# Mask matmuls of the first batch behind both units' scores on 64 rows, and late attention results placed by VectorE and small transfers

## The chip, the cores and the metric

One core of a Trainium2 chip. The metric is device microseconds of one execution; a run's time is the median of its repeated executions. The parts of the core that matter here: TensorE (PE, with PEld for its weight loads), VectorE (DVE), ScalarE (ACT), GpSimd (POOL) and SyncE (SP), whose queue issues most of the transfers. The granted clock is the share of TensorE's full clock that the profile records; "half clock" is a stretch in which it was 0.50. All runs told here were of the fast state, and all gave correct results.

## The reference, cut to what matters

Block-sparse attention, followed by a Fourier mix and a two-layer network, on 4 batches of 8 heads, 768 positions and head size 64.

```python
def _attn_ref(q, k, v, sampled_blocks):           # (4, 8, 768, 64) each
    scores = scale * np.matmul(q, k.transpose(0, 1, 3, 2))
    mask = ...   # near blocks, first and last block row and column, sampled blocks (32 x 32)
    scores = np.where(mask, scores, -1000000000.0)
    attn = softmax(scores)                        # cut: written out in the original
    return np.matmul(attn, v)

# x = attention result as (4, 768, 512)
def _moe_ref(x, w_ch1, w_ch2):
    u = x + np.real(np.fft.fft(np.fft.fft(x, axis=1), axis=2))
    un = (u - mean(u)) / sqrt(var(u) + 1e-6)      # cut
    return u + np.maximum(un @ w_ch1, 0.0) @ w_ch2
```

## The kernel before

Two heads make a pair; there are 4 pairs to a batch, 16 in all. A unit is one key tile of 128 by half of the queries (384) for both heads of a pair. A step does two units: their scores, the exponentials, and the values of the step before. A batch is 24 steps. While the attention of one batch runs, the Fourier mix and the network of the batch before are threaded in.

In the first batch (`n < NP`) the mask is not yet there as a tile, so it is added on TensorE: two bfloat16 matmuls of 24 rows (`NB`) put a large negative number on masked blocks. Later batches multiply by a mask tile on VectorE.

```python
def scores(u):
    ...
    s = ps_s.tile([P, 2, 512], FP32, tag="s", name="s")      # two PSUM buffers
    for i in range(2):                                       # two heads, 64 rows each
        nc.tensor.matmul(s[:, i, 0:HS], kT[D * i:D * i + D, c * P:(c + 1) * P],
                         qT[D * i:D * i + D, half * HS:(half + 1) * HS],
                         start=True, stop=n >= NP)
    if n < NP:
        for i in range(2):
            nc.tensor.matmul(s[:, i, 0:HS], of_k[D * i:D * i + NB, c * P:(c + 1) * P],
                             off_q[D * i:D * i + NB, half * HS:(half + 1) * HS],
                             start=False, stop=True)
    return s
```

The values come out transposed (`o`, head size by queries). ACT copies them to SBUF, TensorE transposes them back (`xt`), and ACT copies that into `x`. I call this a placing; each half of a pair has one.

```python
def values(u):
    ...                                                      # matmuls into o
    if c == C - 1:
        oT = sum_p.tile([P, HS], FP32, tag="oT", name="oT")
        nc.scalar.copy(out=oT, in_=o_of.pop((n, half)))

def place(n, half):
    ...
    xt, at = ps_t.tile([P, 512], FP32, tag="t", name="xt"), bank("t")   # the only buffer "t"
    for c in range(T):                                                  # T = 3
        nc.tensor.transpose(xt[:, c * P:(c + 1) * P], oT[:, c * P:(c + 1) * P], ident)
    nc.scalar.copy(out=x_of[b, half][:, :, j * P:(j + 1) * P], in_=...)
```

In the first batch ACT and DVE also unpack the weights, 32 rounds (`w_round`: two ACT instructions, five DVE instructions, about 3 us of DVE each), and each step issues its short jobs (transposes of q and k, placings) when the kernel's own model thinks that their inputs are ready:

```python
while short and (s in (2, 5) or len(short) > 1 or phase == 0 or r == 0):
    ready = [i for i in short if max(i[1], min(free[i[0]])) <= when["PE"] + 0.1]
    if not ready and s not in (2, 5) and r > 0:
        break
    ...
```

## Time and profile before

| | before |
|---|---|
| time, median of 3 runs | 1109.58 us (1108.61 to 1111.27) |
| span of the profiled run | 1108.8 us, mean granted clock 0.988 |
| PE / DVE / ACT busy | 96% / 60% / 35% |
| longest wait of PE | 4.04 us at 25.27 us |
| first step of the second batch (start of its scores) | 135.41 us |

PE sets the time, so one asks of every change what it takes from PE, and what then stands just behind PE. "Busy" is a share of the whole span.

### The profile page before, as it was taken

How to read it: one execution, taken by the hardware profiler on the slowest of the kernel's cores; microseconds unless marked ns; L12 is line 12 of the kernel's file. 1: busy time of each engine (PE TensorE's matmuls, PEld its weight loads, DVE VectorE, ACT ScalarE, POOL GpSimd, SP SyncE). 2: the span in 40 equal slices, each digit the busy share in tenths (PEclk: the TensorE clock that was granted, in tenths of full speed). 3: DMA queues.
4: the chain of work that ended last, by engine and by line, in shares of the span. 5: the costliest groups of instructions: out<-in, count | busy, mean ns of one | idle time of the engine just before them, and what ended most of it. 6: DMA issues, size and time to landing. Idle time of an engine off the chain costs nothing.

```text
span 1108.8 us, 12273 instructions
## 1 busy us (share of the span) xinstructions
PE 1065.3 (96%) x4370; PEld 537.9 (49%) x4370; DVE 670.6 (60%) x1227; ACT 389.8 (35%) x786; POOL 271.2 (24%) x302
## 2 busy tenths in 40 slices
PE   7999988998899999999999999999999999999996
PEld 4333333443455545444444545444444555568675
DVE  5688878497864535564558635555456446575563
ACT  5788755565202102253443212344330202120210
POOL 1000078487200001245537000343540000000000
PEclk9999999999999999999999999999999999999998
DMA  7557322022000000212210000211000000100001
GB/s 237 151 161 234 109 53 59 15 44 43 1 1 1 1 1 19 62 24 39 43 29 15 0 1 1 55 46 29 1 1 1 0 1 20 38 1 1 1 16 44
DMA packets 86689, 44.28 MB, mean 40 GB/s; under 512 B 74318, under 2 KB 79452, under 8 KB 86620
## 3 DMA queue, kind: packets, MB, share of 16 engines
q1 hardware_dynamic: 84732, 42.62, 14.5%
q10 hardware_dynamic: 1856, 0.79, 0.3%
q8 instruction: 36, 0.59, 0.2%
q14 instruction: 33, 0.27, 0.1%
q0 software_dynamic: 32, 0.01, 0.0%
HBM read 37.11 MB, written 6.29 MB: 39 GB/s over the span
## 4 chain that ended last, share of the span: by engine, by line
PE 83%; DVE 10%; ACT 2%; issue 2%; DMA 1%; POOL 1%; SPq 0%; ACTq 0%; DVEq 0%; POOLq 0%
PE y L1017 23%; PE z L961 14%; PE s L541 10%; PE o L585 8%; PE yp L961 7%; PE yy L1080 6%; PE xp L961 3%; DVE e L562 3%; PE zp L774 1%; PE sp L632 1%; PE zp L745 1%; DMA out_dram<-x 1%; PE xt L603 1%; PE tp L483 1%; DVE w_sb L452 1%
## 5 line engine op out<-in xcount | busy, mean ns | idle before, releaser
L572 POOL TENSOR_TENSOR acc<-acc,e 128x384 f32<-128x384 f32 x192 | 197.4, 1060 | 89.5 <-DVE e L562 88.9
L541 PE MATMUL s<-qT,kT 64*128 64x384 f32 x768 | 164.4, 531 | 15.2 <-DVE e L562 11.0
L562 DVE TENSOR_TENSOR e<-s,mask 128x768 f32<-128x768 f32 x144 | 131.1, 949 | 65.0 <-ACT s L560 62.9
L585 PE MATMUL o<-e,vr 128*64 128x384 f32 x768 | 148.0, 507 | 0.0
L560 ACT ACTIVATE s<-s 128x768 f32<-128x768 f32 x144 | 109.5, 791 | 89.3 <-PE s L541 88.1
L1020 DVE TENSOR_TENSOR x<-y,x 128x512 f32<-128x512 f32 x72 | 49.8, 691 | 146.8 <-PE y L1017 146.7
L1017 PE MATMUL y<-w_sb,hA 128*128 128x512 f32 x288 | 129.5, 595 | 1.1 <-ACT zs L776 1.1
L1017 PE MATMUL y<-w_sb,hB 128*128 128x512 f32 x288 | 128.5, 596 | 1.0 <-DVE x L1020 1.0
L572 POOL TENSOR_TENSOR acc<-e 128x384 f32<-128x384 f32 x48 | 50.0, 1063 | 231.3 <-DVE e L562 189.1
L541 PEld LDWEIGHTS s<-qT,kT 64*128 64x128 f32 x768 | 62.4, 187 | 85.1 <-DVE e L562 37.9
L966 DVE TENSOR_TENSOR hA<-z,hA 128x384 f32<-128x384 f32 x64 | 35.7, 558 | 97.5 <-PE z L961 97.5
L961 PE MATMUL z<-unT,t 128*128 128x384 f32 x256 | 93.0, 486 | 0.0
L837 POOL TENSOR_SCALAR st<-st 128x1 f32<-128x1 f32 x24 | 6.7, 277 | 348.1 <-DVE st L836 347.7
L1017 PEld LDWEIGHTS y<-w_sb,hB 128*128 128x128 f32 x288 | 53.3, 190 | 67.3 <-issue 65.6
L585 PEld LDWEIGHTS o<-e,vr 128*64 128x64 f32 x768 | 47.4, 138 | 75.9 <-issue 72.3
L1017 PEld LDWEIGHTS y<-w_sb,hA 128*128 128x128 f32 x288 | 52.9, 190 | 62.9 <-issue 58.5
L970 ACT ACTIVATE hA<-hA 128x384 f32<-128x384 f32 x64 | 33.5, 523 | 119.9 <-DVE hA L966 119.5
L961 PEld LDWEIGHTS z<-unT,t 128*128 128x128 f32 x256 | 48.6, 190 | 33.9
L970 ACT ACTIVATE hB<-hB 128x384 f32<-128x384 f32 x64 | 33.5, 523 | 86.1 <-DVE hB L966 86.1
L961 PE MATMUL xp<-unT,w_sb 128*128 128x384 f32 x128 | 48.5, 503 | 1.3 <-DVE x L1020 0.7
L981 ACT COPY hA<-xp 128x384 f32<-128x384 f32 x32 | 15.3, 479 | 95.8 <-PE xp L961 95.8
L961 PE MATMUL z<-t,w_sb 128*128 128x384 f32 x128 | 46.6, 487 | 0.9 <-DVE t L923 0.9
(197 smaller groups left out, 1409.1 us busy)
## 6 DMA issues: line engine op xcount, KB each, us to landing
wraw<-in_moe_w_ch_dram SPq DMA_DIRECT2D x32, 512.0 KB
vr<-in_v_dram SPq DMA_DIRECT2D x30, 192.0 KB
qr<-in_q_dram SPq DMA_DIRECT2D x48, 64.0 KB
kr<-in_k_dram SPq DMA_DIRECT2D x14, 192.0 KB
qb<-in_q_dram SPq DMA_DIRECT2D x28, 96.0 KB
kb<-in_k_dram SPq DMA_DIRECT2D x28, 96.0 KB
out_dram<-x SPq DMA_DIRECT2D x16, 128.0 KB
out_dram<-x SPq DMA_DIRECT2D x8, 256.0 KB
```

What stands on the lines that cost most here:

```text
L541: nc.tensor.matmul(s[:, i, 0:HS], kT[D * i:D * i + D, c * P:(c + 1) * P], qT[D * i:D * i + D, half * HS:(half + 1) * HS], start=True, stop ...
L560: nc.scalar.activation(out=s[:, :, 0:HS], in_=s[:, :, 0:HS], func=ACT.Exp, scale=scale)
L562: nc.vector.tensor_tensor(out=e, in0=s[:, :, 0:HS], in1=m.broadcast_to([P, 2, HS]), op=ALU.mult)
L572: nc.gpsimd.tensor_add(out=acc, in0=e_of[u - 1][:, i, :] if c == 1 else acc, in1=e[:, i, :])
L585: nc.tensor.matmul(o[D * i:D * i + D, :], vt[:, i, c, :], e[:, i, :], start=(c == 0), stop=(c == C - 1))
L961: nc.tensor.matmul(to, a[:, k, :], c[:, k, :], start=(k == 0), stop=(k == ND // 2 - 1))
L966: tt(out=to, in0=ps, in1=a, op=ALU.add)
L970: nc.scalar.activation(out=h, in_=h, func=ACT.Relu)
L981: nc.scalar.copy(out=h11, in_=x)
L1017: nc.tensor.matmul(y, hs[0, half][:, l, m * P:(m + 1) * P], w2_sb[:, 4 * r + l, :], start=(l == 0), stop=(l == 3))
L1020: nc.vector.tensor_tensor(out=x[:, m, :], in0=y, in1=x[:, m, :], op=ALU.add)
L1080: nc.tensor.matmul(ps, a[:, k, :], c[k // 2][:, k % 2, :] if isinstance(c, list) else c[:, k, :], start=(k == 0), stop=(k == 3))
```

## The change

Three things, with one aim, fewer microseconds on PE:

1. The mask matmuls of a step stand behind the scores of both units and use 64 rows like the scores (the rows that hold no mask are zeroed once).
2. The transposes of the first pair's second half of q are issued one step earlier (`sl > 1`).
3. From the third batch on, three pairs of four are placed without PE: DVE transposes `o` in blocks of 32 by 32, and 16 small transfers per half put the blocks into `x`. For their sake the loads of q and k are issued earlier in the step.

```diff
+    nc.vector.memset(of_k, 0.0)
+    nc.vector.memset(off_q, 0.0)
...
-    def scores(u):
+    def scores(us):
...
+        for u in us:
+            ...                                   # score matmuls of both units, as before
+        for u, s in got if n < NP else ():
+            for i in range(2):
+                rows = slice(D * i, D * i + D)
+                nc.tensor.matmul(s[:, i, 0:HS], of_k[rows, c * P:(c + 1) * P], off_q[rows, queries],
+                                 start=False, stop=True)
...
+            if in_blocks(n):
+                nc.vector.transpose(out=oT, in_=o_of.pop((n, half)))
...
+    def in_blocks(n):
+        return n > 2 * NP and n % NP > 0
+
+    def place_blocks(n, half):
+        b, j = pairs[n]
+        oT = o_of.pop((n, half)).rearrange("p (c t d) -> p c t d", t=P // BLK, d=BLK)
+        for g in range(P // BLK):
+            for t in range(P // BLK):
+                nc.sync.dma_start(
+                    out=x_of[b, half][BLK * t:BLK * t + BLK, :, j * P + BLK * g:j * P + BLK * (g + 1)],
+                    in_=oT[BLK * g:BLK * g + BLK, :, t, :])
...
-            if not ready and s not in (2, 5) and r > 0:
+            if not ready and s not in (2, 5) and r > 0 and sl > 1:
...                                               # load_q, load_k moved ahead of the short jobs
```

More of the change, by code (lines that the diff above doesn't have):

```diff
@@ L531 @@
     SLOT = 2
-    def scores(u):
-        n, w = divmod(u, UP)
-        half, c = divmod(w, C)
+    def scores(us):
+        n, w = divmod(us[0], UP)
+        half = w // C
         qT, kT = turned[n, 0], turned[n, 1]
-        s = ps_s.tile([P, 2, 512], FP32, tag="s", name="s")
-        busy("PE", 0.72 if n >= NP else 1.0, max(e_at.get(u - SLOT, 0.0), z_at[u % 2]))
-        s_at[u] = when["PE"] + HOP
-        for i in range(2):
-            nc.tensor.matmul(s[:, i, 0:HS], kT[D * i:D * i + D, c * P:(c + 1) * P],
-                             qT[D * i:D * i + D, half * HS:(half + 1) * HS],
-                             start=True, stop=n >= NP)
-        if n < NP:
-            for i in range(2):
-                nc.tensor.matmul(s[:, i, 0:HS], of_k[D * i:D * i + NB, c * P:(c + 1) * P],
-                                 off_q[D * i:D * i + NB, half * HS:(half + 1) * HS],
+        queries = slice(half * HS, (half + 1) * HS)
+        got = []
+        for u in us:
+            c = u % C
+            s = ps_s.tile([P, 2, 512], FP32, tag="s", name="s")
+            got.append((u, s))
+            busy("PE", 0.72, max(e_at.get(u - SLOT, 0.0), z_at[u % 2]))
+            s_at[u] = when["PE"] + HOP
+            for i in range(2):
+                rows = slice(D * i, D * i + D)
+                nc.tensor.matmul(s[:, i, 0:HS], kT[rows, c * P:(c + 1) * P], qT[rows, queries],
+                                 start=True, stop=n >= NP)
+        for u, s in got if n < NP else ():
+            c = u % C
+            busy("PE", 0.25)
+            s_at[u] = when["PE"] + HOP
+            for i in range(2):
+                rows = slice(D * i, D * i + D)
+                nc.tensor.matmul(s[:, i, 0:HS], of_k[rows, c * P:(c + 1) * P], off_q[rows, queries],
                                  start=False, stop=True)
-        return s
+        return got
     def weigh(u, s):
@@ L590, in values @@
             oT = sum_p.tile([P, HS], FP32, tag="oT", name="oT")
-            nc.scalar.copy(out=oT, in_=o_of.pop((n, half)))
-            oT_at[n, half] = busy("ACT", 0.5, when["PE"] + HOP) + HOP
+            if in_blocks(n):
+                nc.vector.transpose(out=oT, in_=o_of.pop((n, half)))
+                oT_at[n, half] = busy("DVE", 0.5, when["PE"] + HOP) + HOP
+            else:
+                nc.scalar.copy(out=oT, in_=o_of.pop((n, half)))
+                oT_at[n, half] = busy("ACT", 0.5, when["PE"] + HOP) + HOP
             o_of[n, half] = oT
@@ L1244, in slot @@
         if sl < B * SB:
-            for u, ps in [(u, scores(u)) for u in units]:
+            for u, ps in scores(units):
                 weigh(u, ps)
@@ L1256, in slot @@
                 e_of.pop(u)
+        if s == 3 and n + 2 < len(pairs):
+            load_q(n + 2)
+        if s == 0 and 0 < n < len(pairs) - 1:
+            load_k(n + 1)
         reuse = n % NP == 0 and phase >= 2
@@ L1264, in slot @@
                 at = when["PE"] + LEAVES
-            short.append(("t", at, lambda: place(n, 0)))
+            if in_blocks(n):
+                place_blocks(n, 0)
+            else:
+                short.append(("t", at, lambda: place(n, 0)))
         if 0 < sl <= B * SB and s == 0 and n % NP != 1:
-            short.append(("t", oT_at[n - 1, 1], lambda: place(n - 1, 1)))
+            if in_blocks(n - 1):
+                place_blocks(n - 1, 1)
+            else:
+                short.append(("t", oT_at[n - 1, 1], lambda: place(n - 1, 1)))
         if sl < B * SB and n % NP == 1 and s == 1:
@@ L1313, in slot @@
                     fn(*args)
-        if s == 3 and n + 2 < len(pairs):
-            load_q(n + 2)
-        if s == 0 and 0 < n < len(pairs) - 1:
-            load_k(n + 1)
         w_loads()
```

## The prediction

> **What bounds the kernel now.** I read the page's busy shares and slices first, then the chain of waits, then the timeline of each stage. The page says that TensorE (PE) is the bound: 96% busy, and the chain that ended last is 83% PE and 10% VectorE (DVE).
>
> ```profile
> PE 1065.3 (96%) x4370; PEld 537.9 (49%) x4370; DVE 670.6 (60%) x1227; ACT 389.8 (35%) x786; POOL 271.2 (24%) x302
> ...
> PE   7999988998899999999999999999999999999996
> ...
> DVE  5688878497864535564558635555456446575563
> ```
>
> So what leaves PE counts in full, except where another engine stands just behind it. In the first five slices (27.7 us each) DVE is that engine: 8 or 9 tenths. This is the first batch, in which DVE also unpacks the weights. The timeline of its start shows the one long wait of PE in the run:
>
> ```profile
> 18.61 0.43 DVE L450 TENSOR_SCALAR wraw<-wraw 128x512 uint32<-128x512 uint32 x1 [8.89 <-ACT wraw L449]
> ...
> 24.57 0.55 DVE L492 COPY qT<-tp 128x128 f32<-128x128 f32 x3
> ...
> 25.27 1.65 PE L541 MATMUL s<-qT,kT 64*128 64x384 f32 x4 [4.04 <-DVE qT L492]
> ```
>
> PE has transposed the second half of q at 18.56, but the copy stands on DVE behind two weight rounds (18.61 to 24.57). PE idles 4.04 us, and its next score matmuls take 1.65 us where others take 0.92. From 32.3 us to 135.4 us PE then has no wait over 0.31 us. One unit's scores, its mask matmuls, the next unit's, and what follows:
>
> ```profile
> 43.93 0.92 PE L541 MATMUL s<-qT,kT 64*128 64x384 f32 x4
> 44.78 0.34 PE L546 MATMUL s<-at_q,at_k 24*128 24x384 bf16 x2
> 45.04 0.92 PE L541 MATMUL s<-qT,kT 64*128 64x384 f32 x4
> 45.89 0.34 PE L546 MATMUL s<-at_q,at_k 24*128 24x384 bf16 x2
> 46.16 1.51 PE L585 MATMUL o<-e,vr 128*64 128x384 f32 x8
> ```
>
> Read the differences of the starts, since the durations overlap: two units take 46.16 - 43.93 = 2.23 us. In the second batch, without mask matmuls, two units take 146.30 - 144.81 = 1.49 us:
>
> ```profile
> 144.81 1.56 PE L541 MATMUL s<-qT,kT 64*128 64x384 f32 x8
> 146.30 0.55 PE L659 MATMUL st<-ident,sums 128*128 128x128 f32 x3
> ```
>
> The first batch ends with DVE late: it works without a gap until its first masked product, and PE waits for that 1.51 us.
>
> ```profile
> 140.19 1.80 DVE L562 TENSOR_TENSOR e<-s,mask 128x768 f32<-128x768 f32 x2
> 141.18 1.78 PE L541 MATMUL s<-qT,kT 64*128 64x384 f32 x8 [1.51 <-DVE e L562]
> ```
>
> From 415 to 840 us, where the other half of the change lies, PE is busy 417.89 of 425 us and DVE 230.51: only PE matters there.
>
> **What the Trainium skill says.** "TensorEngine Tiling (Array Packing)", Key Properties, has it that a change of the tiling mode, not of the tile, drains the engine. The trace agrees: a run of two score passes before a mask takes 0.85 us (43.93 to 44.78), a run of four takes 1.49, so an inner pass is 0.32 and the two ends of a run cost 0.21 together, about 0.10 each. "TensorE: Matmul & The Clock Gate", Part 1, gives half clock after an idle window of about 3.4 us; here the 4.04 us wait is followed by matmuls at half speed until about 31 us. "VectorE: DVE Perf Modes", The three transpose paths, says that DVE transposes only within 32x32 blocks; hence the 16 transfers per half, which put the blocks in place. "DMA: Bandwidth & Descriptors", Rules for kernel authors, warns that transfers under 64 KB are mostly overhead; these are 12 KB. No transfer like them is in this trace, so their time is my least certain input.
>
> **The change, part by part.**
>
> *Mask matmuls.* 24 steps of two units. Now the mask pair has 24 rows, a different mode from the scores' 64, so a step has four runs. Afterwards it is one run of 64 rows: four score passes, then two mask pairs. A mask pair at the end of a run takes 0.26 (45.89 to 46.16), thus about 0.16 inside one. If nothing but rows matters, a step takes 1.49 - 0.10 + 0.16 + 0.26 = 1.81: 0.42 saved. If the step from f32 to bf16 drains as well, 1.91: 0.32 saved; if each mask's weights wait too, 2.01: 0.22. I take 0.35, 8.4 us over the batch. The exponentials on ScalarE (ACT) of the first unit start about 0.9 us later; the values that read them come a step later, so this should be hidden.
>
> *The early copy.* The order of instructions shows that the q transpose moves ahead of the third step's scores, and its copy ahead of all weight rounds on DVE. The 4.04 us go, and half clock from 25.3 to 31 us, 5.7 us at half speed: 2.9 us. A new wait comes: this transpose now directly follows another in the same single PSUM buffer, which ACT must empty first (six copies, 1.03 us, which start after the exponentials). Laying the recorded durations in the new order gives the third step's scores at about 17.9 us instead of 16.33, then the fifth step's at about 26.9, against 32.33 plus the 0.48 of a placing transpose that now stands ahead of it: some 6.0 us gained, the masks of the first four steps included. The other 20 steps bring 20 x 0.35 = 7.0: PE would reach the second batch 13.0 us earlier.
>
> *What DVE makes of this.* From its weight round at 62.08 us to the masked product at 140.19 DVE has only about 4.8 us idle (gaps of 1.55, 1.44 and 1.80); before, it has gaps of 4.37, 4.14 and 3.13. All are waits for ACT or PE, which come earlier too, so most of them close; but its first weight round starts some 1.5 us later, behind the square of q on ACT. I put DVE's end at 127.5 to 128.5 us, 12 us earlier; PE waits there 2.5 us instead of 1.5. Gain at the second batch: 11.8 us. Its PE, DVE and ACT orders are otherwise unchanged, so the shift is kept.
>
> *Late placing.* Six pairs, two halves: 12 placings. Each takes 3 PE transposes away, 0.48 us (156.23 to 156.71), 5.7 us in all, and waits in front of some of them, the largest 1.42 us at 578 and 0.85 us here:
>
> ```profile
> 837.16 0.52 PE L603 MATMUL xt<-ident,oT 128*128 128x128 f32 x3 [0.85 <-DVE sums L616]
> ```
>
> I count 1.5 us of these. 24 ACT copies of 0.48 us go too, which PE does not wait for. Added: 12 DVE transposes of 128x384; the one of 128x768 takes 968 ns, so about 0.5 us each, 6 us on an engine a little over half busy; and 192 transfers. A 1 to 63 row transfer holds the queue for about 0.26 to 0.32 us, so I estimate 16 in about 5.5 us, landing 2 us later. The next use of the same buffer is three steps, over 20 us, later. Loads stand in the same queue, but the change issues q and k ahead of them, and v is needed a pair later. The last placing matters most: it stores into x at the end of the attention part. DVE scales x there:
>
> ```profile
> 842.24 1.29 DVE L674 TENSOR_TENSOR x<-x,r 128x512 f32<-128x512 f32 x2
> 844.91 0.69 DVE L1020 TENSOR_TENSOR x<-y,x 128x512 f32<-128x512 f32 x1 [1.38 <-PE y L1017]
> 845.52 1.89 DVE L674 TENSOR_TENSOR x<-x,r 128x512 f32<-128x512 f32 x3
> ```
>
> Only the second half of x is concerned, from the middle of the last line on, 846 us; with values done at 835.5, the transpose at 836.1 and 7.5 us of transfers it is there at about 844. PE has second-layer matmuls of the batch before to do meanwhile. No cost, narrowly.
>
> *Sum.* 11.8 + 5.7 + 1.5 = 19.0. I take off 1 us for half clock: waits of 2.48 and 2.18 us in the second batch were followed by 3.4 us windows at half speed, and the DVE wait at the batch's border may now be one of those. Net 18 us: 1109.6 - 18 = 1091.6 us.
>
> **Rivals.** (1) *DVE becomes the bound of the first batch and swallows the masks' gain.* For: 87.11 us busy in the 103 us from 34 to 137 and late already at the end. Against: 10 us of gaps that are waits for others. If they stay open, the first batch gains only some 7 us, and the time is about 1096. (2) *bf16 behind f32 drains anyway, and ACT gets bursts.* ACT is 84.55 of 103 us busy and takes two exponentials in a row later than now; the two score buffers could make PE wait for it. Worth 3 to 5 us: 1095. (3) *The small transfers hold up the queue or the last x.* If one costs 0.6 us of queue as the q loads do (3.82 us for 6), 16 take 10 us, the last x is 3 to 4 us late, and PE loses some of it: 1094. (4) *All works, DVE's gaps close fully and waits at xt go too*: 14 + 8 = 22 us, 1087.5, right at the border of 2%.
>
> **Range and chances.** The sure pieces are the start's wait (at least 4 us) and 12 placings (5.7 us): no less than about 10 us. Everything together gives 22 to 23. Hence 1087 to 1098 for 8 in 10. 2% is 22.2 us, 1087.4: only rival 4 gets there, 0.13. Slower by 2% needs a long new wait that nothing suggests: 0.01.
>
> **What would show it.** In the first batch, two units' scores with masks 1.8 to 1.9 us apart from start to the values' start (2.0 or more: drains remain); no wait of 4 us before 26 us, one of about 1 us at the transpose near 17 us, and no half clock; the first step without masks at 122 us instead of 135.4, and the PE wait at its second step at 2 to 4 us, for DVE e (10 us would mean rival 1). DVE's gaps between 28 and 123 us, about 17 us in all now, shrink to 8 or less. The placing transposes fall from 96 to 60, and the stretch from 415 to 840 us becomes 6 to 7 us shorter. A DVE or PE wait for the transfers near the end of attention would prove rival 3. I am wrong in the main if the first batch gains under 8 us.

## The result, and the profile after

| | before | after |
|---|---|---|
| time, median (same rounds, 4 runs each) | 1110.09 us (1108.61 to 1111.27) | 1093.09 us (1091.21 to 1095.11) |
| span of the profiled run, clock | 1108.8 us, 0.988 | 1089.3 us, 0.993 |
| start of the second batch's 1st / 2nd / 3rd step | 135.41 / 141.18 / 144.81 | 122.80 / 129.33 / 134.21 |
| placing transposes on PE | 96 | 60 |

The ratio is 0.9848 (95% interval 0.9826 to 0.987). All ratios here compare runs of the same rounds, so they are not quite the ratios of the medians. All outputs are right. The verdict at 2% is "same": 17.0 us, 1.5%, against a predicted 18 us.

The page of the kernel after, busy shares, DVE's row of the slices and the chain that ended last:

```profile
PE 1048.1 (96%) x4334; PEld 534.4 (49%) x4334; DVE 675.3 (62%) x1241; ACT 379.1 (35%) x762; POOL 270.2 (25%) x302
...
DVE  5899887598745524664567536554556355575663
...
PE 83%; DVE 9%; ACT 3%; issue 2%; DMA 2%; POOL 1%; SPq 0%; ACTq 0%; DVEq 0%; POOLq 0%
```

PE is busy 17.2 us less, of the 19.5 us by which the two spans differ; its share stays 96%, so it is still the bound. DVE's second digit of the slices has gone from 6 to 8: its work of the first batch has fewer gaps.

The timeline at the start (start, duration, engine and line, what waited in brackets). The long wait for DVE is gone, and a shorter one for ACT stands at the q transposes, as ACT must first empty their only PSUM buffer:

```profile
15.83 0.66 PE L486 MATMUL tp<-ident,qk 128*128 128x128 f32 x4
...
17.60 0.44 PE L486 MATMUL tp<-ident,qr 128*128 128x128 f32 x2 [1.12 <-ACT qT L495]
```

One step with masks. From the start of the scores to what follows the masks it takes 47.77 - 45.95 = 1.82 us, where two units took 2.23 before:

```profile
45.95 1.56 PE L551 MATMUL s<-qT,kT 64*128 64x384 f32 x8
47.34 0.49 PE L559 MATMUL s<-at_q,at_k 64*128 64x384 bf16 x4
47.77 0.66 PE L486 MATMUL tp<-ident,qr 128*128 128x128 f32 x4
```

The border of the first two batches: DVE works through its last weight rounds (L461 is the end of one) and only then reaches the first masked product, for which PE waits 2.27 us:

```profile
122.80 1.56 PE L551 MATMUL s<-qT,kT 64*128 64x384 f32 x8
...
129.33 2.93 PE L551 MATMUL s<-qT,kT 64*128 64x384 f32 x8 [2.27 <-DVE e L574]
...
134.21 1.56 PE L551 MATMUL s<-qT,kT 64*128 64x384 f32 x8
```

```profile
127.20 0.69 DVE L461 TENSOR_TENSOR w_sb<-w_sb,wraw 128x512 f32<-128x512 f32 x1
...
128.34 1.80 DVE L574 TENSOR_TENSOR e<-s,mask 128x768 f32<-128x768 f32 x2
```

The scores at 129.33 last 2.93 us instead of 1.56. The view of windows (a line has the window, its length, the busy time and count of PE, PEld, DVE, ACT and POOL, granted clock, DMA) shows why: half clock, 0.50.

```profile
129.00:132.40 3.40, 3.07 (x10) 1.34 (x12) 2.15 (x4) 0.88 (x2) 1.94 (x2) 0.50 0.00 0
```

The small transfers: durations as minimum, median and maximum in ns from the view of the tile oT, with DVE's block transposes; and then from the timeline the last half's 16 transfers, DVE's wait for them, the end of the folds of x, and the first matmul that needs the folds:

```profile
L635 SPq DMA_DIRECT2D x<-oT x192: 585/597/1324, 468.8 to 827.4; - x192
...
L604 DVE STREAM_TRANSPOSE oT<-o x12: 571/571/582, 468.2 to 817.2; 128x384 f32<-128x384 f32 x12
```

```profile
817.80 10.25 SPq L635 DMA_DIRECT2D x<-oT  x16
```

```profile
829.55 1.29 DVE L705 TENSOR_TENSOR x<-x,r 128x512 f32<-128x512 f32 x2 [2.91 <-DMA x<-oT]
...
842.53 0.16 DVE L756 COPY sd<-sd 128x3 f32<-128x3 f32 x1
```

```profile
845.34 1.46 PE L776 MATMUL zp<-cs_sb,sa 128*128 128x385 f32 x4
```

Here a transfer holds the queue for about 0.64 us on average (10.25 us for 16), twice my estimate. DVE waits 2.91 us for the last ones; but the folds are done at 842.5 and the matmul that uses them comes at 845.3 in its turn, with no wait on it: PE lost nothing.

### The profile page after: what moved, and what is told of

Its sections match the earlier page's. It is cut to its first block, busy times and chain, and to the rows that moved or that the text cites. A ratio compares the mean times of both kernels' runs of the same rounds, so it can differ in the third digit from the quotient of the medians.

```text
span 1089.3 us, 12419 instructions
## 1 busy us (share of the span) xinstructions
PE 1048.1 (96%) x4334; PEld 534.4 (49%) x4334; DVE 675.3 (62%) x1241; ACT 379.1 (35%) x762; POOL 270.2 (25%) x302
## 4 chain that ended last, share of the span: by engine, by line
PE 83%; DVE 9%; ACT 3%; issue 2%; DMA 2%; POOL 1%; SPq 0%; ACTq 0%; DVEq 0%; POOLq 0%
PE y L1048 23%; PE z L992 15%; PE s L551 10%; PE o L597 8%; PE yp L992 7%; PE yy L1111 6%; PE xp L992 3%; DVE e L574 3%; PE zp L805 2%; PE sp L663 1%; PE zp L776 1%; DMA out_dram<-x 1%; DVE x L855 1%; POOL acc L584 1%; PE tp L486 1%
## 5 line engine op out<-in xcount | busy, mean ns | idle before, releaser
L551 PE MATMUL s<-qT,kT 64*128 64x384 f32 x768 | 157.4, 523 | 13.9 <-DVE e L574 12.1
L597 PE MATMUL o<-e,vr 128*64 128x384 f32 x768 | 145.5, 500 | 0.0
L1051 DVE TENSOR_TENSOR x<-y,x 128x512 f32<-128x512 f32 x72 | 49.7, 690 | 139.4 <-PE y L1048 139.3
L992 PE MATMUL yp<-unT,w_sb 128*128 128x384 f32 x128 | 46.9, 489 | 0.4 <-DVE un L841 0.4
```

Source lines behind the costliest of these rows:

```text
L551: nc.tensor.matmul(s[:, i, 0:HS], kT[rows, c * P:(c + 1) * P], qT[rows, queries], start=True, stop=n >= NP)
L597: nc.tensor.matmul(o[D * i:D * i + D, :], vt[:, i, c, :], e[:, i, :], start=(c == 0), stop=(c == C - 1))
L992: nc.tensor.matmul(to, a[:, k, :], c[:, k, :], start=(k == 0), stop=(k == ND // 2 - 1))
L1051: nc.vector.tensor_tensor(out=x[:, m, :], in0=y, in1=x[:, m, :], op=ALU.add)
```

## The experiments

Times of profiles are compared step by step. Since the starts of the runs differ by up to 1 us, a step's time is counted from the first step's first score matmul of the same profile; counted so, the changed kernel reaches the second batch's second step 11.96 us before the kernel before it. Numbered steps are counted from 0 over the whole run, so that step is step 25.

| run | what | median us | ratio to before (95%) |
|---|---|---|---|
| masks_only | part 1 alone | 1106.22 | 0.9975 (0.9958 to 0.9991) |
| early_only | part 2 alone | 1103.61 | 0.9945 (0.9929 to 0.9962) |
| placing_only | part 3 alone | 1104.80 | 0.9965 (0.9947 to 0.9984) |
| rows_24_behind | all, masks with 24 rows | 1095.18 | 0.9866 (0.9848 to 0.9885) |
| after_again | the changed kernel | 1093.84 | 0.986 (0.983 to 0.989) |
| rows_64_each | all, masks behind each unit | 1091.63 | 0.9844 (0.9815 to 0.9872) |
| pool_add | all, one add of a weight round on GpSimd | 1097.74 | 0.9894 (0.9865 to 0.9923) |
| act_first | all, ACT empties o ahead of the block transpose | 1094.84 | 0.9864 (0.9836 to 0.9893) |
| fill_wait | all, PE kept busy in the border's wait | 1092.21 | 0.9839 (0.9825 to 0.9852) |
| late_rounds | all, two weight rounds moved to steps 38, 39 | 1096.92 | 0.988 (0.9865 to 0.9895) |
| late_and_bank | the last, and another buffer for q | 1095.09 | 0.9862 (0.9847 to 0.9877) |
| late_bank_more | the last, and six more placings | 1094.00 | 0.9858 (0.9843 to 0.9873) |

They ran in three groups of four, in the order of the table, each beside the kernel before, which took 1108.75, 1110.84 and 1109.89 us (medians of 7, 7 and 9 runs). Times of different groups are compared by their ratios.

My theory at the start: the parts add up, with DVE's backlog of weight rounds standing just behind PE at the border of the first two batches. The rival: they don't add up, because DVE swallows most of what the masks give.

**The three parts alone.** In masks_only:

```diff
+ scores(us) with the 64-row masks behind both units, and the two memsets
- everything else of the change
```

> The kernel before with only the mask matmuls moved and widened to 64 rows. Both theories: two units' scores with masks take 1.81 us instead of 2.23, so TensorE loses 24 x 0.42 = 10 us of work; the 4 us wait for the q copy at 21 us stays. Theory A (VectorE's weight rounds stand just behind TensorE, so part of the gain turns into a longer wait at the second batch's second step): that step starts 7 to 8 us earlier than before's 141.18, the wait before it is 3 us or more instead of 1.5, and the time falls by 6 to 8 us. Theory B (TensorE alone counts): 10 us at that step and in the time, the wait stays at 1.5 us.

In early_only:

```diff
-            if not ready and s not in (2, 5) and r > 0:
+            if not ready and s not in (2, 5) and r > 0 and sl > 1:
```

> The kernel before with only the q transpose and its copy moved ahead. Both theories: no wait of 4 us and no half clock before 31 us, a new wait of about 1.1 us for the one PSUM buffer. Theory A: the second batch's second step starts 5 to 6 us earlier, and masks_only and this one together give more than the 11.9 us (141.18 to 129.33) that both changes give at that step, since both draw on the same gaps of VectorE. Theory B: their gains at that step add up to 11.9 us.

In placing_only:

```diff
+ in_blocks, place_blocks, the transposes on DVE, the earlier loads
- everything else of the change
```

> The kernel before with only the late placing by VectorE and transfers (and the loads issued ahead of it). If TensorE's work is what counts: 36 transposes fewer, 12 x 0.48 = 5.7 us, and about 2 us of waits in front of them, 7 to 8 us less time, though VectorE waits some 3 us for the last transfers. Rival, that the transfers cost TensorE something: 4 us or less.

Counted in steps, masks_only reaches the second batch's second step 6.8 us earlier and early_only 5.9 us. The sum, 12.7, is 0.8 us more than both together give (11.96). That difference arises in the first four steps (1.52 + 5.06 us against 5.83 at the start of the fifth), where both parts work on the same wait and half clock; from there to the border they add up to within 0.02 us. What DVE takes is read at the border itself: PE's wait there grew from 1.51 to 2.27 us in masks_only, as in the changed kernel, and stayed at 1.51 in early_only. So DVE takes 0.8 us of the masks' gain, not most of it. I had expected more, a wait of 3 us and 7 to 8 us at this step. The line of each part that carries it:

```profile
135.19 2.93 PE L551 MATMUL s<-qT,kT 64*128 64x384 f32 x8 [2.27 <-DVE e L574]
```

```profile
18.02 0.44 PE L483 MATMUL tp<-ident,qr 128*128 128x128 f32 x2 [1.12 <-ACT qT L492]
```

The first line (masks_only) is the border's wait with half clock behind it, without the early copy. The second (early_only) is the new wait for ACT, which therefore comes with the early issue and not with the masks.

In time the parts gave less: masks_only 2.5 us, where I had expected 6 to 8, early_only 5.1, and placing_only 4.0, which is what its rival had named (4 us or less). Half clock accounts for most of it: the four runs of masks_only had mean granted clocks of 0.985 to 0.988 and those of placing_only 0.987 to 0.990, where five of the seven runs of the kernel before in this group had 0.990. A run's span times its mean clock is a rough measure of its time at full clock; it averages 1089.6 us for masks_only and 1090.0 for placing_only against 1095.5, so 5.9 and 5.5 us less. That is near the steps. Why these two kernels fall to half clock more often was not tested.

placing_only gained 6.7 us between steps 56 and 95, of which 1.6 are a half-clock period at 737.5 us that the kernel before has there and this run lacks, and 1.1 us after them: 6.1 without that period, where I had expected 7 to 8. The starts of neighbouring PE groups before show why. Three placings with different neighbours (o, scores; y, scores; z, yp, where y, z and yp belong to the network of the batch before):

```profile
482.51 0.55 PE L603 MATMUL xt<-ident,oT 128*128 128x128 f32 x3
482.99 1.24 PE L541 MATMUL s<-qT,kT 64*128 64x384 f32 x6
```

```profile
519.10 0.49 PE L603 MATMUL xt<-ident,oT 128*128 128x128 f32 x3
519.52 1.56 PE L541 MATMUL s<-qT,kT 64*128 64x384 f32 x8
```

```profile
555.79 0.49 PE L603 MATMUL xt<-ident,oT 128*128 128x128 f32 x3
556.12 1.13 PE L961 MATMUL yp<-t,w_sb 128*128 128x384 f32 x3
```

Three transposes take 0.48 us between values and scores, which have other modes of the array (the 128\*64 and 64\*128 that the lines print), but 0.33 where both neighbours have the same mode (128\*128), as then no change of mode goes with them. In the second case even 0.09 of the 0.42 comes back: y to scores takes 0.52 us without a placing, 0.43 to the placing with one, so 0.33 is saved. Summed over the 12, the transposes are worth 4.6 us and not 12 x 0.48 = 5.7. With 2.3 us of waits that makes 6.9 us; about 0.6 us comes back (the first y matmul behind values is 0.1 us longer without a placing ahead of it, four times; and the scores behind the sums where the larger wait was take 0.2 us longer), which leaves 6.3. The changed kernel against masks_only, in which only the placing differs late in the run, gives 4.95 us between steps 56 and 95 and 1.2 after: 6.1. So, counted in steps, the gain adds to the others in full.

**What in the masks' new form saves the time?** In rows_24_behind the masks stand behind both units, with 24 rows:

```diff
-                rows = slice(D * i, D * i + D)
+                few = slice(D * i, D * i + NB)
```

> The changed kernel with the mask matmuls still behind both units' scores, but on 24 rows as before. If the change of the row count drains the engine: two units take 1.91 us instead of 1.81, a mask run starts 0.41 us after the last score pass instead of 0.32. If rows do not matter and only the fewer alternations do: 1.81. In the time the 24 x 0.10 = 2.4 us shows only in part, 0 to 2 us slower than the changed kernel, since VectorE bounds the end of the first batch.

In rows_64_each they stand behind each unit's own scores, with 64 rows:

```diff
+            if n < NP:                     # inside the loop over the units
+                matmuls of of_k[rows], off_q[rows] into this unit's s
-        for u, s in got if n < NP else ():
```

> The changed kernel with 64-row masks, but each unit's mask straight behind its own scores, as before. If only the row count counts (24 rows drain, f32 to bf16 does not): two units still 1.81 us, and the time within 1 us of the changed kernel. If standing behind both units' scores matters by itself: 1.97 us or more, some 4 us slower.

> The changed kernel once more, as the mark for the other runs on this chip: 1091 to 1095 us, two units with masks 1.81 us apart, a wait of about 2.3 us before the second batch's second step.

The same step in both, rows_24_behind first:

```profile
47.19 1.56 PE L551 MATMUL s<-qT,kT 64*128 64x384 f32 x8
...
49.11 0.66 PE L486 MATMUL tp<-ident,qr 128*128 128x128 f32 x4
```

```profile
44.75 0.92 PE L551 MATMUL s<-qT,kT 64*128 64x384 f32 x4
...
46.57 0.66 PE L486 MATMUL tp<-ident,qr 128*128 128x128 f32 x4
```

49.11 - 47.19 = 1.92 with 24 rows, 46.57 - 44.75 = 1.82 with 64 in the old order, 1.82 in the changed kernel and in after_again. For the length of a step the row count is all there is to it: from the last score matmul to the mask it takes 0.316 us at 64 rows, the same as between two score passes, though the type changes from f32 to bfloat16, and 0.415 us at 24 rows. The old order with 24 rows changed the rows three times inside a step (2.23 us), the new order changes them once (1.92), with 64 rows they never change (1.82). So going from 64 to 24 rows costs 0.10 us, and coming back 0.21.

The order is not quite without effect, and here it speaks for the old one: rows_64_each reaches the fifth step 0.8 us before the changed kernel and the second batch 0.9 us before it. With the masks behind both units ACT's first exponential starts later (1.79 us after the first scores, not 1.14), and PE waits for it and for ACT's copy behind it before the second step's scores (0.29 and 0.16 us); rows_64_each has neither wait. rows_24_behind reaches the second batch 1.7 us after the changed kernel, of 2.4 us that 24 steps would give. In time none of the three can be told from another: their intervals overlap.

**DVE at the border.** In pool_add, GpSimd, idle in the first batch, takes the last of a weight round's five DVE instructions:

```diff
-        nc.vector.tensor_add(out=dst, in0=dst, in1=a.bitcast(FP32))
+        nc.gpsimd.tensor_add(out=dst, in0=dst, in1=a.bitcast(FP32))
```

> The changed kernel with the last add of each of the 32 weight rounds on GpSimd, idle in the first batch, instead of VectorE: 22 us less for VectorE there. If VectorE's lateness is what is left between the masks' gain and the time: the 2.3 us wait before the second batch's second step falls under 0.5 us, no half clock follows it, and the time is 2 to 4 us below the changed kernel's. Rival, GpSimd slows VectorE or delays the weights: the wait stays, the same time or slower.

It is slower than the changed kernel. The view of the tile wraw, in pool_add:

```profile
L455 DVE SCALAR_TENSOR_TENSOR w_sb<-wraw x32: 691/1635/1655, 21.3 to 129.6; 128x512 uint32<-128x512 uint32 x32
L458 DVE TENSOR_SCALAR wraw<-w_sb x32: 426/427/429, 22.0 to 131.2; 128x512 uint32<-128x512 uint32 x32
...
L461 POOL TENSOR_TENSOR w_sb<-w_sb,wraw x32: 1263/1379/1397, 23.3 to 132.5; 128x512 f32<-128x512 f32 x32
```

The add left DVE (0.69 us), but the instruction of the next round that runs beside it on DVE, with two tensors as inputs, grew from a median of 0.69 to 1.64 us. L458 kept its 0.43, but it never ran beside an add. L453, which has one tensor as input, did so 23 times: the 17 that had started before the add took 0.42 us, the 6 that started after it 1.25 to 1.34, and these 6 all ended 0.29 us after their add. So the one that comes second waits for the first. The Trainium skill has this, "SBUF — State Buffer", Who interferes with whom: a DVE instruction with two SBUF inputs contends with a GpSimd instruction that reads SBUF. This trace agrees (1.64 us against 0.69). PE's wait at the border rose to 5.07 us. Work that leaves a full engine is no gain if it then holds that engine up.

**The wait of the value matmuls for the block transpose.** The trace after shows 2.7 us in which PEld waits for DVE's transposes to free the PSUM buffer of `o`. In act_first ACT empties it, and DVE transposes in SBUF:

```diff
-                nc.vector.transpose(out=oT, in_=o_of.pop((n, half)))
+                nc.scalar.copy(out=oT, in_=o_of.pop((n, half)))
+                nc.vector.transpose(out=oT, in_=oT)
```

> The changed kernel with the late sums taken out of PSUM by ScalarE, as before, and then transposed in place by VectorE in SBUF. In the changed kernel TensorE waited 2.7 us in five places for VectorE's transposes to free the one PSUM buffer of the sums. If that is what the placing gives back: these waits vanish and the stretch of the last two batches is 2 to 2.7 us shorter. Rival: the same time, because 12 more ScalarE copies and the later transfers cost as much.

The waits vanished, and nothing came of it: steps 64 to 68 take 23.40 us in both, 88 to 92 also 23.40, 92 to 95 19.22 in both. I was wrong here. The wait was the weight load's alone; the matmuls behind it came no later with it than without it. A wait of PEld is not a wait of PE.

**The half clock behind the border's wait.** In fill_wait PE does useless matmuls there:

```diff
+        if sl == SB + 1:
+            m = ps_t.tile([P, P], FP32, tag="t", name="fill")
+            for _ in range(8):
+                nc.tensor.matmul(m, ident, ident, start=True, stop=True)
```

> The changed kernel with eight matmuls of no use in front of the scores of the second batch's second step, where PE idles 2.27 us for VectorE and then runs 3.4 us at half clock. Theory A (the idle stretch itself brings the half clock): the fill shortens the idle to about 0.8 us, there is no half-clock window from 129 to 132.4 us, the step after it takes about 3.6 us (as in the kernel before) instead of 4.88, and the run gains about 1.3 us: 1092 or so. Rival B (the half clock comes from something else, for instance the change of the work at the batch's border): the window stays and the step still takes 4.9 us.

PE's timeline at the border, and a later window of that run:

```profile
127.14 2.05 PE L1278 MATMUL fill<-ident 128*128 128x128 f32 x16 [0.57 <-ACT x L620]
129.13 1.56 PE L551 MATMUL s<-qT,kT 64*128 64x384 f32 x8
...
132.53 1.56 PE L551 MATMUL s<-qT,kT 64*128 64x384 f32 x8
```

```profile
139.40:142.80 3.40, 3.40 (x13) 1.20 (x11) 0.96 (x1) 2.52 (x6) 0.75 (x1) 0.50 0.17 39
```

Theory A holds at the place: without the idle stretch there is no half clock, and the step takes 3.40 us instead of 4.88. But a new half-clock stretch stands at 139.4, behind two waits of 0.86 and 1.12 us that the changed kernel has too, without half clock after them:

```profile
136.88 0.63 PE L486 MATMUL tp<-ident,qr 128*128 128x128 f32 x4 [0.86 <-issue]
138.62 0.44 PE L486 MATMUL tp<-ident,qr 128*128 128x128 f32 x2 [1.12 <-ACT qT L495]
```

The time (1092.21) is not to be told from the changed kernel's.

This made me lay all 14 profiles side by side. Between the warm-up and the end, all the recorded half-clock stretches of a profile start on one grid of 3.413 us, to within 0.01 of a period, and last one or two periods. I summed PE's idle time in each period of that grid that ran at full clock. Of 55 periods with over 1.87 us idle, all 55 were followed by half clock; of 55 with 1.0 to 1.7 us, none was; between, 7 of 16. So about half a period of idle time is the threshold, and the grid's position, which differs from execution to execution, decides whether two waits of 0.86 and 1.12 fall in one period or in two. In a period already at half clock less is enough: all 8 with 0.84 us idle or more were followed by another one, none of 62 with 0.68 or less. A period costs at most about 1.7 us (an estimate, half of 3.41); at 737.5 us it cost 1.6. The Trainium skill, "TensorE: Matmul & The Clock Gate", Part 1, knows the free-running window of 3413 ns, and the grid agrees; it has half clock after an idle window, and these profiles show that a window need be idle for only about half of its length. That this is also where the spread of 4 us between the runs of one kernel comes from fits (the changed kernel's four runs had clocks of 0.993, 0.992, 0.989 and 0.988 at spans of 1089.3, 1091.1, 1091.2 and 1093.1 us), but no run controlled it.

**Taking the backlog itself away.** In late_rounds the last two weight rounds go into idle stretches of DVE in the second batch; the order on PE is unchanged:

```diff
-            w_round(state["w"])
+            if state["w"] < len(wchunks) - 2:
+                w_round(state["w"])
...
+        if 38 <= sl < 40:
+            w_round(len(wchunks) - 40 + sl)
```

> The changed kernel with the last two weight rounds (3 us of VectorE each) taken out of the first batch and done at steps 38 and 39, where VectorE has idle stretches of 3.8 and 7.8 us; the order on PE stays as it is. Theory A (the wait at the batch's border is VectorE's backlog and nothing else, and the half clock follows from the wait): the first batch's end doesn't move (122.8 us), the second step comes at about 127.1 instead of 129.3, with no half clock behind it the third at 130.7 instead of 134.2, and the 3.5 us are kept: 1089 to 1090. Rival B (behind VectorE stands something else, such as the exponentials on ACT or the sums): the step comes less than 1 us earlier. Rival C (the rounds cost PE at steps 38 and 39 what they gave): a wait of 2 us or more there.

In late_and_bank also the q transposes' second PSUM buffer:

```diff
-        tag, pool = ("m", ps_m) if first and a == 0 else ("t", ps_t)
+        tag, pool = ("m", ps_m) if n == 0 and a == 0 else ("t", ps_t)
```

> The last one with the transposes of the first q's second half in another PSUM buffer, so that they needn't wait until ACT has emptied the one before. Theory A (the new wait of 1.12 us at 17.6 us comes only from that buffer): it goes, the later steps of the first batch come about 1.1 us earlier, and as VectorE is no longer the bound at the border, so does the rest: 1088 to 1089. Rival B: the copies on ACT or VectorE come no sooner and the next scores wait for them instead: under 0.4 us.

In late_bank_more also the second batch's later pairs by transfers:

```diff
-        return n > 2 * NP and n % NP > 0
+        return n > NP and n % NP > 0
```

> The last one with the second batch's three later pairs placed by transfers too (18 placings instead of 12). Theory A (PE's saving per placing is 0.33 to 0.48 us by what stands beside it, also where PE isn't saturated, and the queue is hidden): six placings give 1 to 2.5 us: 1086 to 1088. Rival B (in the second batch PE waits for others, so that its work is hidden, or the 10.5 us of queue for each half hold up loads there): 0 to 0.5 us, or slower.

At the border of late_rounds PE runs on without a wait, and the second batch's third step comes 3.85 us earlier than in the changed kernel:

```profile
126.45 1.56 PE L551 MATMUL s<-qT,kT 64*128 64x384 f32 x8
...
129.86 1.56 PE L551 MATMUL s<-qT,kT 64*128 64x384 f32 x8
```

That is theory A: the border's wait is DVE's backlog. But the run ended 4.7 us slower than fill_wait of the same group, as rival C had it. The moved rounds stood in front of masked products. PE's scores of step 41, then the start of DVE's first moved round and the product that stood behind the second:

```profile
211.10 2.93 PE L551 MATMUL s<-qT,kT 64*128 64x384 f32 x8 [3.58 <-DVE e L574]
```

```profile
199.83 0.43 DVE L453 TENSOR_SCALAR wraw<-wraw 128x512 uint32<-128x512 uint32 x1 [8.25 <-ACT wraw L452]
...
210.09 1.81 DVE L574 TENSOR_TENSOR e<-s,mask 128x768 f32<-128x768 f32 x2
```

By step 42 the 3 us gained had become 3 us lost, with half clock from 211.1. The first of DVE's two lines says why: the idle stretch of 8.25 us was there, but the round begins with ACT's part, which stood behind ACT's other work of the step; so it started only when the idle stretch was over. Whether a step earlier, or a later stage, would keep the 3 us was not run.

In late_and_bank the wait of 1.12 us is gone, and the next scores wait 0.68 us for ACT instead:

```profile
20.76 1.62 PE L551 MATMUL s<-qT,kT 64*128 64x384 f32 x8 [0.68 <-ACT e L569]
```

From step 3 to step 38 all steps come 0.6 us earlier than in late_rounds: between A (1.1) and B (under 0.4). late_bank_more is 5.3 us ahead of late_and_bank at step 38, and 0.3 us at step 56: in the second batch PE waits for others, and the work taken off it was largely hidden, as rival B said. Its time is 1.1 us better, and its profile had fewer half-clock periods than late_and_bank's, so this settles nothing. No version that I ran is shown to be faster than the changed kernel.

## Why the prediction was right or wrong

- *Masks.* The mechanism was right and the size low: 0.42 us per step came, the best of the options named, and not 0.35. The drain from f32 to bfloat16, which I had allowed for, doesn't exist at equal rows. Over 20 steps that is 8.4 us instead of 7.0; most of the surplus was given back, as PE idles 1.74 us between the fifth and the 25th step, where it idled 0.41 before (1.0 us of it are new waits for ACT's exponentials, which rival 2, with the drain, had put at 3 to 5); so the gain between these steps came out as 6.9, next to the 7.0 predicted. That it came so close is luck: two errors cancel.
- *The early copy.* Predicted 26.9 us for the fifth step, measured 26.61. The new wait, predicted at about 1 us, was 1.12. That the first unit's later exponentials are hidden was not quite so: they cost the early steps 0.8 us, as rows_64_each shows.
- *What DVE makes of it.* Predicted 11.8 us at the border and a wait of 2.5 us; measured 11.85 and 2.27. DVE's gaps shrank to about 4 us of 95. Rival 1 (DVE swallows the gain) is refuted: the wait at the border grew by 0.76 us, and that is what DVE took. (The gaps that rival 1 puts at 10 us are 12 in the stretch that it names; nothing hangs on it.)
- *Half clock.* I took off 1 us for it; the stretch at the border cost 4.88 - 3.63 = 1.25 us. The amount was good, but my reading that it takes an idle window of about 3.4 us was not, as the grid shows; my own sum already went by waits of 2.48 and 2.18 us.
- *Late placing.* The failed term of the sum is "Each takes 3 PE transposes away, 0.48 us (156.23 to 156.71), 5.7 us in all": I had measured one placing, between two changes of mode, and taken it for all. They were worth 4.6 us. The waits, counted at 1.5 us, were 2.3, and about 0.6 us came back: 6.1 in the runs instead of 7.2.
- *Transfers.* The other failed term: 16 transfers held the queue for 10.25 us, not 5.5; rival 3 had named 0.6 us each. My test for that rival, "A DVE or PE wait for the transfers near the end of attention would prove rival 3", came true with DVE's 2.91 us and proved only half of it: the transfers are late, but PE had other work until 845.3 us. The test should have named PE alone.
- *Sum.* 11.85 + 6.1 - 1.25 = 16.7 us, against 17.0 in the medians. The two profiles differ by 19.5, because the profiled run of the changed kernel was its fastest, with three half-clock periods, and that of the kernel before had six, two of which belong to the removed wait. The predicted 1091.6 lies 1.5 us below the median of 1093.09.

## What to carry to other kernels

A small matmul between others costs what it does to the array's mode: make its rows equal to its neighbours', and its place among them no longer changes the length of the step (it can still change who waits for what); and take its price from several of its places, not from one. A part's gain should be counted step by step in the trace, since half-clock periods of up to 1.7 us each, which depend on how idle stretches fall, can hide it in the time. Before moving work into another engine's idle stretch, look where in that engine's order it will really stand, and whom it holds up there.

## What the Trainium skill lacked or had wrong

- "TensorE: Matmul & The Clock Gate", Part 1: it has half clock after an idle window of about 3.4 us. Half a window is enough: in 14 profiles every one of 55 full-clock periods of the 3.413 us grid with over 1.87 us of PE idle was followed by half clock, none of 55 with 1.0 to 1.7.
- "TensorEngine Tiling (Array Packing)", Key Properties: a change of mode drains, but no figure is given: here going from 64 rows to 24 costs 0.10 us and coming back 0.21. It doesn't say that a change of the data type at equal rows costs nothing, which these runs show (0.316 us from the last f32 score pass to the first bfloat16 mask, the same as between score passes).
- "DMA: Bandwidth & Descriptors", Rules for kernel authors: no time measured on trn2 for how long a small SBUF-to-SBUF transfer holds its queue: here 12 KB held the SP queue for 0.585 us at least, 0.597 in the median, and 16 in a row for 10.2 us and more.
- "VectorE: DVE Perf Modes", The three transpose paths: only a figure for bfloat16; 128x384 of f32 from PSUM took 571 ns.
